# Empty TensorE instructions that move seven joined phases against lines of 256 instructions, and states' products first in four of them

## The chip, the cores and the metric

The kernel runs on one core of one Trainium2 chip. The metric is the device time of one execution in microseconds (us); lower is better. The core's engines run side by side, each through its own stream of instructions, and wait for each other by semaphores: TensorE (PE in the profile; its weight loads are PEld), VectorE (DVE), ScalarE (ACT), GpSimd (POOL) and SyncE (SP), which here starts nearly all DMAs. The median of three runs before the change is 552.23 us (550.72 to 553.09).

## What is computed

A linear-attention block, whose state decays step by step, is followed by a two-layer feed-forward block.

```python
# attention: r, k, v, w of (B=4, H=8, S=768, D=48), u of (H, D)
for t in range(S):
    cur = einsum('bhd,bhe->bhde', u[None] * kt, vt)
    y[:, :, t] = einsum('bhd,bhde->bhe', rt, state + cur)
    state = wt[:, :, :, None] * state + einsum('bhd,bhe->bhde', kt, vt)
x = y.transpose(0, 2, 1, 3).reshape(3072, 384)
# feed-forward: w_in of (384, 2048), w_out of (2048, 384)
h = x @ w_in
out = (h - tanh(h)) @ w_out
```

## The kernel before

**Blocks.** The 3,072 tokens are cut into eight blocks of 384 (`NB`): four sequences (`b`) of two halves (`q`). Loop `i` over the blocks runs the feed-forward part of block `i` and, between its steps, prepares the attention part of block `i + 1` (`later`). The attention of block 0 is done ahead, in `boot`.

**Feed-forward.** Inside a block, `f` runs over the 16 tiles of 128 hidden units. `first` (line 868) makes three matmuls, one for each 128 rows of `x`, into `hp`; its matmul is line 870. ACT copies `hp` to `h` (line 873), ACT and DVE make the activation `g` from it, and some tiles later the second layer consumes `g`. The second layer is done plainly in block 0 (`Second.add`, line 944, its matmul at line 947; in the last tiles of block 7 by `Second.added`, line 972) and by a scheme with fewer products in the others (`Fewer.product`, line 994), whose operands (`forms`, and sums of `g` tiles, line 917) DVE adds up. What is due is kept in the list `due`: the second layer of tile `f` is issued three tiles later in block 0, and from two tiles later on in the others.

**Attention.** A block is computed by chunks of 64 tokens (`L`). The products within a chunk form scores (line 493), which DVE copies under a mask to `A` (line 501) and to whose diagonal it copies another term (`diagonal_in`, line 396). The states at the chunks' starts come from products (line 574) that DVE adds and scales step by step (line 586). At tile 13 of blocks 0 and 1 and at tile 12 of blocks 2 to 6, `together` (line 731) joins both: `stretch` is called for `scores` and then for `from_state`, twice each, and makes up to 24 calls of a small matmul each time, all by line 756. In this text such a call of `together` is the joined phase of block `i`: it stands in the stream of block `i`, with the data of block `i + 1`. Where `later` is the first half of a sequence (`q` is 0, so `i` is 1, 3 or 5) the first chunk has no tokens ahead of it and the phase is shorter. ACT copies its results to `xT` and `late` (line 728), and small DMAs fill `xT` up.

Every matmul in float32 with line 870, 947, 994 or 756 stands in the profile as two matmuls and two weight loads. Thus three calls of line 870 make "x6".

**What sets the order.** PE, SP, DVE and ACT run in the order in which the program names their instructions; the order is written out by hand. In a tile `f` of a block, PE's order is: `first`, then phases of the attention part (line 493 or 574), then what is due of the second layer, then, in its tile, the joined phase. Where an instruction waits for more semaphores than it can hold, a separate semaphore instruction stands ahead of it in PE's stream. Behind the main part a branch leads, for inputs that don't keep to bounds checked on the way, to a general version of the whole computation (`general`), which also calls `first` and `Second.add`; with these inputs it isn't run.

Of the kernel before, what the change touches and what calls it, by code (L numbers as in the profile page):

```python
# [53 lines left out]
NB = 384  # L54
# [14 lines left out]
NF = FF // P  # L69
# [7 lines left out]
UNITS = [(0, 0), (0, 1)] + [u for j in range(NF // 2 - 2) for u in ((1, j), (0, j + 2))] + [(1, NF // 2 - 2),  # L77
                                                                                      (1, NF // 2 - 1)]
LATE = 3

# [43 lines left out]
def kernel(  # L126
# [12 lines left out]
    nc = tc.nc  # L139
# [76 lines left out]
    sums = const.tile([P, 16, P], F32, name="sums", tag="sums")  # L216

    def ring(t, at, n):
        return t[:, at + n % 4 * 3:at + n % 4 * 3 + 3].rearrange("p t c -> p (t c)")
# [3 lines left out]
    def g_at(q, x):  # L223
        if not isinstance(x, str):
# [9 lines left out]
    n_whole = blocks_n * NPAIR * NCH  # L234
    light = [n for n in range(blocks_n * NF) if NF - LATE <= n < blocks_n * NF - 2 and
             (n < NF or few[n // NF])]
# [76 lines left out]
    def begin_behind(ins, then):  # L313
        tc.add_manual_dep(then.ins, ins.ins.name, mybir.DependencyInfo(
            mybir.DependencyClass.Sync, mybir.DependencyReason.DATA))
# [3 lines left out]
    class Block:  # L319
# [411 lines left out]
        def together(self, ps):  # L731

            self.results(ps)
            yp, spread, St, ended = self.yp, isinstance(ps, Kept), states[self.q], {}

            def scores(p, c, h, par):
                toks = slice(64 * par, 64 * par + 64)
                return self.v[toks, c, p * D2 + h * D:p * D2 + (h + 1) * D], A[toks, h, p, c, :]

            def from_state(p, c, h, par):  # L740
                rows = slice(64 * h, 64 * h + D)
                return St[rows, p, 2 * c + par, 0:D], self.chunk("pre", p, 2 * c + par, spread)[rows]

            def stretch(of, cross):
                first = cross not in ended
                begun = set()
                for n in range(UP):
                    for c in range(NCP):
                        for h in range(2):
                            for x in range(2):  # L750
                                p, par = UP * n + x, x ^ cross
                                if of is from_state and not (self.q or c or par):
                                    continue
                                lhs, rhs = of(p, c, h, par)
                                e0, n0 = 64 * (h ^ x), (n * NCP + c) * L
                                done = nc.tensor.matmul(yp[x][e0:e0 + D, par, n0:n0 + L], lhsT=lhs, rhs=rhs,  # L756
                                                        start=first and (x, e0) not in begun, stop=True,
                                                        skip_group_check=True)
                                begun.add((x, e0))
                                if not first and len(begun) == 1:  # L760
                                    begin_behind(ended[cross], done)
                if first:
                    ended[cross] = nc.gpsimd.memset(ended_at, 0.0)
                    begin_behind(done, ended[cross])

            for of in (scores, from_state):
                for cross in range(2):
                    stretch(of, cross)
            self.result_out(ALL)
            self.fill_holes([nc.sync])  # L770
# [94 lines left out]
                self.update_any(ps, p0, self.tots[L])  # L865
            self.together(ps)

    def first(xT, f, hp):
        for kc in reversed(range(KC)):
            nc.tensor.matmul(hp, lhsT=w_in_sb[:, f, kc, :], rhs=xT[kc],  # L870
                             start=(kc == KC - 1), stop=(kc == 0))
        h = dense.tile([P, NB], F32, name="h", tag="h")
        return h, nc.scalar.activation(out=h, in_=hp, func=AF.Copy, scale=1.0 / UPSCALE)  # L873

    def product(out, in0, scalar, in1, op0):
        return lambda: nc.vector.scalar_tensor_tensor(out=out, in0=in0, scalar=scalar, in1=in1,  # L876
                                                      op0=op0, op1=ALU.mult)
# [42 lines left out]
    def any_h(h, g):  # L920
        s, qa = (dense.tile([P, NB], F32, name=name, tag=name) for name in ("s", "qa"))
        th, qb, big = (inp.tile([P, 2 * HALF], F32, name=name, tag=tag)[:, 0:NB]
                       for name, tag in (("th", "k"), ("qb", "r"), ("big", "w")))
        nc.scalar.activation(out=s, in_=h, func=AF.Square)
        nc.scalar.activation(out=qa, in_=s, func=AF.Square, bias=shift[:, 0:1])
        nc.scalar.activation(out=qb, in_=s, func=AF.Square, bias=shift[:, 1:2])
        nc.scalar.activation(out=th, in_=h, func=AF.Tanh)
        nc.scalar.activation(out=big, in_=s, func=AF.Relu, bias=shift[:, 2:3])
        nc.vector.tensor_tensor(out=th, in0=h, in1=th, op=ALU.subtract)
        product(h, h, SERIES, s, ALU.mult)()  # L930
        product(h, qa, QUAD[0][1], h, ALU.add)()
        product(g, qb, QUAD[1][1], h, ALU.add)()
        nc.vector.copy_predicated(out=g, mask=big.bitcast(I32), data=th)
        return g

    def places(at, n):
        return sums[:, at:at + n].rearrange("p n c -> p (n c)")

    class Second:
# [1 line left out]
        def __init__(self, row0, acc, first=0):  # L941
            self.row0, self.acc, self.first = row0, acc, first

        def add(self, f, g):
            for j in range(NB // P):
                acc = self.acc[j][:, 0:DM]
                nc.tensor.matmul(acc, lhsT=g[:, j * P:(j + 1) * P], rhs=w_out_sb[:, f, :],  # L947
                                 start=(f == self.first), stop=(f == NF - 1))
                if f == NF - 1:
                    rows = slice(self.row0 + j * P, self.row0 + j * P + P)  # L950
                    if rows.stop == N:
                        for at, engine in ((slice(0, DM // 2), nc.scalar), (slice(DM // 2, DM), nc.vector)):
                            o = places(12, 3)[:, at]
                            if engine is nc.scalar:
                                nc.scalar.activation(out=o, in_=acc[:, at], func=AF.Copy, scale=1.0 / UPSCALE)
                            else:
                                nc.vector.tensor_single_scalar(o, acc[:, at], 1.0 / UPSCALE, op=ALU.mult)
                            queue = nc.scalar if engine is nc.scalar else nc.sync
                            queue.dma_start(out=out[rows, at], in_=o)
                        continue  # L960
                    o = dense.tile([P, DM], F32, name="o", tag="o", bufs=2) if j < 2 else places(12, 3)
                    nc.scalar.activation(out=o, in_=acc, func=AF.Copy, scale=1.0 / UPSCALE)  # L962
                    nc.sync.dma_start(out=out[rows, :], in_=o)
# [245 lines left out]
    xT = blocks[0].begin()  # L1209
# [32 lines left out]
    for i, blk in enumerate(blocks):  # L1242
        here = xT
        later = blocks[i + 1] if i + 1 < len(blocks) else None
        after = blocks[i + 2] if i + 2 < len(blocks) else None
        if later:
            xT = later.begin()
# [3 lines left out]
        second = Second(row0, acc, few[i]) if few[i] < NF else None  # L1251
        for f in range(NF):
# [2 lines left out]
                op()  # L1255
            spare_a, spare_b = (t[:, 0] for t in ps_a.both)
            to = [acc[0], acc[1], hp, spare_a, spare_b, spare_a][now] if now < 6 else hp
            h, made = first(here, f, to[:, 0:NB])
            if not i:
                made_up = converting(pieces, (PIECES[f] if f < len(PIECES) else 1) - 1)  # L1260
                for op in ahead_of_h:
# [2 lines left out]
            g, ahead_of_h, square, later_ops = slight(h, now, i, f)  # L1264
            some = ({4: (0, 2), 6: (2, 4), 8: (4, 6), 9: (6, 8), 14: (8, len(SUMS))} if later else
                    {4: (0, 4), 6: (4, 8), 8: (8, len(SUMS))}).get(f) if summed else None
            spare = summed[0].sum(*some) if some else []
# [76 lines left out]
            for name in loads.get(f, ()):  # L1344
                of, ins = (after if name in ("w", "k", "r") else later), None
# [34 lines left out]
    with tc.If(anew > 0, label="anew"):  # L1380
        with tc.manual_schedule(engines={PE, SP, DVE, ACT}), ExitStack() as again_pools:
            ps_d = again_pools.enter_context(tc.tile_pool(name="ps_e", bufs=1, space=PSUM))
            ps_a = again_pools.enter_context(tc.tile_pool(name="ps_b", bufs=2, space=PSUM))
            acc = [ps_d.tile([P, BANK], F32, name=f"acc{j}", tag=f"acc{j}") for j in range(NB // P)]
            hp = ps_d.tile([P, NB], F32, name="hp", tag="hp")
            draw((1, 2, 4, 8), slice(128, 288))
            for st in states:
                nc.vector.memset(st[:, :, :, D:], 0.0)
            for blk in [Block(b, q) for b in range(B) for q in range(NQ)]:
                blk.general(ps_a)  # L1390
                second = Second(blk.b * S + blk.q * NB, acc)
                for f in range(NF):
                    second.add(f, any_h(first(blk.xT, f, hp)[0], ring(sums, 0, f)))


# [52 lines left out]
```

## Time and profile before

| | |
|---|---|
| median of 3 runs | 552.23 us (550.72 to 553.09) |
| profiled execution | 552.88 us; span 551.1 us |
| PE busy | 536.8 us (97%), 5,682 matmuls |
| PEld busy | 404.7 us (73%) |
| DVE busy | 459.3 us (83%) |
| ACT busy | 403.6 us (73%) |
| granted TensorE clock | 0.995 mean |
| DMA | 56.29 MB, mean 102 GB/s |

The span runs from the first to the last instruction of the profiled execution, whose time lies a little above the median of the three runs. A row of a group or timeline names line, engine, operation and tile (out<-in), and in brackets or behind a bar the idle time ahead with what ended it. "issue" there means that the engine waited for nothing that the profile shows. The rows by stage give, for each engine, busy microseconds and the count of instructions, then the granted clock, the DMA engines' busy share and GB/s. "PEldq" marks instructions that PE's sequencer runs itself.

### The profile page before, as it was taken

The page shows a single profiled execution, that of the slowest core. Times are in us where ns is not written, and L with a number is a line of the kernel's source. Part 1 is how long each engine was busy: PE and PEld are TensorE (multiplying, and loading weights), DVE is VectorE, ACT ScalarE, POOL GpSimd, SP SyncE. Part 2 cuts the span into 40 slices and gives each one's busy share as a digit, 9 for nine tenths or more (in the row PEclk, how much of TensorE's full clock was granted, in tenths as well). Part 3 has the DMA queues.
Part 4 walks back from the last instruction along what each step waited for, and adds up shares of the span by engine and source line. Part 5 has one row for each costly group of instructions (what it writes and reads, how often), then busy time and mean ns, then how long its engine had stood idle before and what let it go on. Part 6 is the DMA issues. An engine that isn't in the chain of part 4 may idle for free.

```text
span 551.1 us, 14091 instructions
## 1 busy us (share of the span) xinstructions
PE 536.8 (97%) x5682; PEld 404.7 (73%) x5682; DVE 459.3 (83%) x943; ACT 403.6 (73%) x814; POOL 6.5 (1%) x47
## 2 busy tenths in 40 slices
PE   8999989999999999999999999999999999999996
PEld 5756655677777787878777787777877777787874
DVE  7899997899979989799897889879787897557563
ACT  5899975897568886688666887588855986666561
POOL 1100000000000000000000000000000000000000
PEclk9999998999999999999999999999999999999999
DMA  7798632252302532144112532126222320200101
GB/s 273 256 398 320 216 116 70 86 129 75 118 11 87 113 113 92 57 122 138 61 55 50 139 117 66 50 87 160 66 86 63 82 63 2 56 0 1 45 1 46
DMA packets 53045, 56.29 MB, mean 102 GB/s; under 512 B 21488, under 2 KB 50928, under 8 KB 52976
## 3 DMA queue, kind: packets, MB, share of 16 engines
q1 hardware_dynamic: 52592, 55.18, 32.8%
q8 instruction: 45, 0.74, 0.6%
q14 instruction: 24, 0.20, 0.1%
q10 hardware_dynamic: 288, 0.10, 0.1%
q0 software_dynamic: 96, 0.07, 0.1%
HBM read 44.73 MB, written 4.72 MB: 90 GB/s over the span
## 4 chain that ended last, share of the span: by engine, by line
PE 92%; DVE 4%; issue 2%; DMA 1%; SPq 0%; DVEq 0%
PE hp L870 43%; PE acc L994 26%; PE att L994 6%; PE acc L947 5%; PE att L756 4%; PE att L493 2%; PE acc L972 2%; PE att L574 2%; PE att L870 1%; DMA r<-in_rT 1%; PE acc L870 1%; DVE scores L501 1%; DVE first_states L630 0%; DVE pre L416 0%; DVE w_sb L267 0%
## 5 line engine op out<-in xcount | busy, mean ns | idle before, releaser
L870 PE MATMUL hp<-xT,w_sb 128*128 128x384 f32 x738 | 260.1, 489 | 0.0
L870 PEld LDWEIGHTS hp<-xT,w_sb 128*128 128x128 f32 x738 | 132.1, 191 | 69.4 <-issue 0.3
L994 PE MATMUL acc<-forms,g 128*128 128x128 f32 x954 | 133.2, 276 | 0.0
L873 ACT ACTIVATE h<-hp 128x384 f32<-128x384 f32 x123 | 60.2, 489 | 98.8 <-PE hp L870 98.3
L994 PEld LDWEIGHTS acc<-forms,g 128*128 128x128 f32 x954 | 122.0, 192 | 10.3
L876 DVE SCALAR_TENSOR_TENSOR h<-h,s 128x384 f32<-128x384 f32 x128 | 70.6, 551 | 60.4 <-ACT s L891 60.4
L917 DVE TENSOR_TENSOR g<-g 128x256 f32<-128x256 f32 x265 | 103.1, 418 | 7.4 <-PE acc L994 6.5
L892 ACT ACTIVATE qa<-s,shift 128x384 f32<-128x384 f32 x113 | 69.5, 615 | 3.7
L894 ACT ACTIVATE junk<-s,shift 128x384 bf16<-128x384 f32 x113 | 67.7, 599 | 0.0
L876 DVE SCALAR_TENSOR_TENSOR g<-qa,h 128x384 f32<-128x384 f32 x112 | 61.5, 550 | 1.6 <-ACT qa L902 0.2
L891 ACT ACTIVATE s<-h 128x384 f32<-128x384 f32 x113 | 59.1, 523 | 3.6
L994 PEld LDWEIGHTS acc<-w_sb,g 128*128 128x128 f32 x318 | 46.8, 191 | 9.7 <-ACT sums L962 0.3
L994 PE MATMUL acc<-w_sb,g 128*128 128x128 f32 x318 | 53.0, 276 | 0.0
L994 PE MATMUL att<-w_sb,g 128*128 128x128 f32 x212 | 35.5, 275 | 0.0
L994 PEld LDWEIGHTS att<-w_sb,g 128*128 128x128 f32 x212 | 31.1, 192 | 5.3
L947 PE MATMUL acc<-w_sb,sums 128*128 128x384 f32 x96 | 34.6, 498 | 0.2 <-DVE sums L876 0.2
L1029 DVE TENSOR_TENSOR sums<-sums 128x256 f32<-128x256 f32 x84 | 32.7, 405 | 1.7 <-ACT sums L1006 1.4
L263 ACT ACTIVATE up<-raw 128x768 f16<-128x768 f32 (+1 forms) x32 | 32.9, 1061 | 0.0
L947 PEld LDWEIGHTS acc<-w_sb,sums 128*128 128x128 f32 x96 | 18.6, 196 | 13.5 <-DVE sums L876 1.1
L416 DVE TENSOR_TENSOR_SCAN pre<-w,start 128x780 f32<-128x780 f32 x14 | 24.9, 1782 | 0.8
L428 DVE TENSOR_TENSOR_SCAN post<-w,seed 128x780 f32<-128x780 f32 x14 | 24.8, 1775 | 0.0
L894 ACT ACTIVATION_READ_ACCUMULATOR junk<-s,shift 128x1 f32 x113 | 21.1, 187 | 0.0
(118 smaller groups left out, 530.1 us busy)
## 6 DMA issues: line engine op xcount, KB each, us to landing
raw<-in_weights SPq DMA_DIRECT2D x16, 768.0 KB, 6.3
w<-in_wT SPq DMA_DIRECT2D x7, 780.0 KB, 4.5
k<-in_kT SPq DMA_DIRECT2D x7, 768.0 KB, 4.7
r<-in_rT SPq DMA_DIRECT2D x7, 768.0 KB, 4.5
v_sb<-in_v SPq DMA_DIRECT2D x8, 576.0 KB, 4.0
k<-in_tokens SPq DMA_DIRECT2D x7, 576.0 KB, 3.9
r<-in_tokens SPq DMA_DIRECT2D x7, 576.0 KB, 4.7
out_y<-sums SPq DMA_DIRECT2D x18, 128.0 KB, 1.8
```

The lines of the kernel that those rows point to most:

```text
L263: return lambda: nc.scalar.activation(out=to, in_=of, func=AF.Copy, scale=scale, bias=bias)
L416: return nc.vector.tensor_tensor_scan(out=self.tile("pre")[:, cols], data0=self.tile("w")[:, cols], data1=start[:, 0:n * NCH * LP], initia ...
L870: nc.tensor.matmul(hp, lhsT=w_in_sb[:, f, kc, :], rhs=xT[kc], start=(kc == KC - 1), stop=(kc == 0))
L873: return h, nc.scalar.activation(out=h, in_=hp, func=AF.Copy, scale=1.0 / UPSCALE)
L876: return lambda: nc.vector.scalar_tensor_tensor(out=out, in0=in0, scalar=scalar, in1=in1, op0=op0, op1=ALU.mult)
L891: nc.scalar.activation(out=s, in_=h, func=AF.Square)
L892: nc.scalar.activation(out=qa, in_=s, func=AF.Square, bias=shift[:, 4:5])
L894: nc.scalar.activation(out=junk[:, 0:NB], in_=s, func=AF.Relu, bias=shift[:, 5:6], accum_out=excess[:, at:at + 1])
L917: return lambda: nc.vector.tensor_tensor(out=G[:, to:to + 2], in0=two(G, g_at(q, a0), g_at(q, a1)), in1=two(G, g_at(q, b0), g_at(q, b1)), ...
L947: nc.tensor.matmul(acc, lhsT=g[:, j * P:(j + 1) * P], rhs=w_out_sb[:, f, :], start=(f == self.first), stop=(f == NF - 1))
L994: nc.tensor.matmul(to, lhsT=G[:, g_at(q, a), :], rhs=rhs, start=start, stop=stop, skip_group_check=True)
L1029: ops.append(lambda op=op, at=at: nc.vector.tensor_tensor(out=at[0], in0=at[1], in1=at[2], op=OPS[op]))
```

## The change

Three things are edited. A table `SPACED` gives, for each block, how many empty instructions (`nc.tensor.nop`) `first` issues behind each of its three matmuls: one number for the tiles up to 13 (blocks 0 and 1) or 12 (the others), one for the tiles behind. `Second.add` issues one behind each of its matmuls in block 0 for tiles 0 to 10. The two calls in the general version ask for none. In `together`, `from_state` goes ahead of `scores` where `self.q` is 1, that is in blocks 0, 2, 4 and 6; elsewhere the order stays.

```diff
+SPACED = (3, 0), (0, 3), (3, 2), (2, 3), (3, 2), (2, 3), (3, 0), (0, 0)
...
-            for of in (scores, from_state):
+            for of in (from_state, scores) if self.q else (scores, from_state):
                 for cross in range(2):
                     stretch(of, cross)
...
-    def first(xT, f, hp):
+    def first(xT, f, hp, apart=0):
         for kc in reversed(range(KC)):
             nc.tensor.matmul(hp, lhsT=w_in_sb[:, f, kc, :], rhs=xT[kc],
                              start=(kc == KC - 1), stop=(kc == 0))
+            for _ in range(apart):
+                nc.tensor.nop(nofuse=True, hint="apart")
...
-        def add(self, f, g):
+        def add(self, f, g, spare=True):
             for j in range(NB // P):
                 acc = self.acc[j][:, 0:DM]
                 nc.tensor.matmul(acc, lhsT=g[:, j * P:(j + 1) * P], rhs=w_out_sb[:, f, :],
                                  start=(f == self.first), stop=(f == NF - 1))
+                if self.row0 == 0 and f < NF - 5 and spare:
+                    nc.tensor.nop(nofuse=True, hint="apart")
...
-            h, made = first(here, f, to[:, 0:NB])
+            h, made = first(here, f, to[:, 0:NB], SPACED[i][f > 12 + (i < 2)])
...
-                    second.add(f, any_h(first(blk.xT, f, hp)[0], ring(sums, 0, f)))
+                    second.add(f, any_h(first(blk.xT, f, hp)[0], ring(sums, 0, f)), False)
```

## The prediction

> **What bounds the kernel now.** I read the page first, for the chain of work that ended last; then the list of what TensorE (PE) waited for.
>
> ```profile
> PE 92%; DVE 4%; issue 2%; DMA 1%; SPq 0%; DVEq 0%
> ```
>
> ```profile
> PE att L756 <- issue: 4.8, 4, 1.7
> ...
> PE att L756 <- DVE scores L396: 1.4, 1, 1.4
> ```
>
> PE is the bound nearly everywhere, so time taken from it reaches the end. Behind the start-up its waits are almost all in one place: line 756, the joined phases, of which there are seven, one in each of blocks 0 to 6. Four of them hold a wait for "issue", time in which nothing that the profile shows was missing; one holds a wait for VectorE (DVE). The timeline of PE has the places (start, length, count; the idle time ahead in brackets), first in block 0, then the rows that end the other three waits.
>
> ```profile
> 75.19 2.20 PE L947 MATMUL acc<-w_sb,sums 128*128 128x384 f32 x6 [0.19 <-DVE sums L876]
> 78.82 1.56 PE L756 MATMUL att<-scores,v_sb 64*48 64x64 f32 x96 [1.43 <-DVE scores L396]
> 80.20 1.41 PE L756 MATMUL att<-pre,states 48*48 48x64 f32 x85
> 83.26 0.42 PE L756 MATMUL att<-pre,states 48*48 48x64 f32 x11 [1.66 <-issue]
> ...
> 150.26 0.59 PE L756 MATMUL att<-pre,states 48*48 48x64 f32 x23 [1.08 <-issue]
> ...
> 276.03 0.42 PE L756 MATMUL att<-pre,states 48*48 48x64 f32 x10 [0.71 <-issue]
> ...
> 405.43 0.44 PE L756 MATMUL att<-pre,states 48*48 48x64 f32 x15 [1.35 <-issue]
> ```
>
> All four fall near the end of a phase, with 11, 23, 10 and 15 matmuls to go. Is the distance between them regular in instructions? The view of busy time by stage counts matmuls (PE) and weight loads (PEld) from one such end to the next, and the view of a line lists the separate semaphore instructions, here between the second and the third (x6, x2, x2) and between the first and the second (x3, x2).
>
> ```profile
> 83.26:150.26 67.00, 65.93 (x638) 47.31 (x637) 60.74 (x121) 50.49 (x107) 0.58 (x5) 0.97 0.35 98
> 150.26:276.03 125.77, 125.06 (x1403) 98.51 (x1403) 111.10 (x228) 94.67 (x199) 0.64 (x8) 1.00 0.31 87
> 276.03:405.43 129.40, 128.05 (x1403) 100.71 (x1403) 111.47 (x232) 95.95 (x202) 0.64 (x8) 1.00 0.32 89
> ```
>
> ```profile
> L870 PEldq EVENT_SEMAPHORE  x6: 51/51/198, 154.2 to 220.9; - x6
> ...
> L994 PEldq EVENT_SEMAPHORE  x2: 51/51/51, 169.7 to 233.5; - x2
> ...
> L574 PEldq EVENT_SEMAPHORE  x2: 51/51/51, 199.5 to 263.4; - x2
> ...
> L870 PEldq EVENT_SEMAPHORE  x3: 51/51/51, 87.4 to 92.1; - x3
> ...
> L994 PEldq EVENT_SEMAPHORE  x2: 51/51/51, 103.6 to 103.7; - x2
> ```
>
> 1,403 + 1,403 + 10 = 2,816 = 11 x 256, twice; and 638 + 637 + 5 is 1,280 = 5 x 256. No larger number divides both. So each wait ends exactly where a new line of 256 instructions begins. The view of DMA from 401 to 408 us shows that line arriving (40 slices of 0.175 us).
>
> ```profile
> GB/s 369 211 114 0 0 0 0 0 94 0 0 0 0 0 0 0 0 0 0 0 0 0 0 0 0 0 0 0 0 0 0 94 0 0 0 0 0 0 0 0
> ...
> q8 instruction: 2, 0.03, 2.3%
> ```
>
> Two instruction packets: one at about 402.5, 2.9 us ahead of the resumption at 405.43; the next at about 406.5, 1.1 us behind it. Entering a line thus seems to ask for the following one, which is usable about 4 us later. Ordinary lines last far longer. A joined phase does not:
>
> ```profile
> 146.74:150.78 4.04, 2.96 (x177) 2.74 (x176) 3.94 (x9) 1.06 (x3) 0.18 (x2) 1.00 0.02 6
> 208.64:211.47 2.83, 2.83 (x194) 2.75 (x193) 2.83 (x6) 1.06 (x3) 0.18 (x2) 1.00 0.06 15
> 272.60:276.38 3.78, 3.07 (x177) 2.84 (x176) 3.78 (x8) 1.06 (x3) 0.18 (x2) 1.00 0.02 5
> 337.51:340.34 2.83, 2.83 (x193) 2.75 (x193) 2.83 (x6) 1.06 (x3) 0.18 (x2) 1.00 0.03 9
> 401.47:405.80 4.33, 2.98 (x177) 2.75 (x177) 4.33 (x10) 1.07 (x3) 0.18 (x2) 1.00 0.02 4
> 466.93:469.76 2.83, 2.83 (x194) 2.75 (x193) 2.21 (x6) 1.06 (x3) 0.18 (x2) 1.00 0.03 6
> ```
>
> A clean phase issues 192 pairs, 384 instructions, in 2.83 us: 7.4 ns each, so a line wholly inside it is eaten in 1.9 us. Phases 1, 3 and 5 have 176 pairs, 352 instructions (the first 64 tokens of a sequence have none ahead of them). From the matmuls left, the boundary stalls at instruction 384 - 22 = 362 of phase 0, and 306, 332 and 322 of phases 1, 3 and 5; the line before begins 256 earlier, at 106, 50, 76 and 66: inside. For the clean phases the same count runs from the last boundary to the phase:
>
> ```profile
> 150.26:208.50 58.24, 58.23 (x517) 45.55 (x517) 51.88 (x107) 45.49 (x96) 0.14 (x2) 1.00 0.32 88
> 276.03:337.36 61.33, 61.33 (x522) 47.85 (x522) 51.81 (x109) 46.76 (x99) 0.14 (x2) 1.00 0.35 94
> 405.43:466.78 61.35, 61.35 (x527) 47.88 (x527) 50.77 (x109) 44.68 (x95) 0.00 (x0) 1.00 0.21 55
> ```
>
> With five waits each (one block, half of the ten above), 1,039, 1,049 and 1,059 instructions, that is 15, 25 and 35 over a multiple of 256: the line began that far ahead of the phase, the next lies 241, 231 and 221 inside, and one more, 256 on, does not fit. No line is wholly inside, and there is no wait. Fifteen slow instructions ahead are enough.
>
> **The empty instructions: where they put the phases.** Each takes one place in PE's stream and no array. Counted from the diff, ahead of phase 0 come 14 first-layer tiles x 3 matmuls x 3 = 126 and 11 second-layer tiles x 3 = 33: 159. Tiles 14 and 15 of block 1 add 18, each of blocks 2, 4 and 6 adds 13 x 9 = 117 ahead of its phase, blocks 3 and 5 add 78, and the tails add 18, 27, 18, 27. Ahead of phases 0 to 6 that makes 159, 159, 294, 390, 534, 630 and 774. The first boundary inside (106, 50, 241, 76, 231, 66, 221) moves forward by as much, modulo 256: to 203, 147, 203, 198, 209, 204 and 215. Every line that holds the start of a phase then begins 41 to 109 instructions ahead of it, and the second boundary, 256 on, lies beyond 384 everywhere. So all four waits should go, and the three clean phases stay clean with more room than before.
>
> **What that is worth.** Phases 1, 3 and 5 should take 2.83 x 352/384 = 2.59 us, and take 4.04, 3.78 and 4.33: 1.45 + 1.19 + 1.74 = 4.4 us. Behind phase 0 the clock falls as well; the chain in order of time has the first-layer matmuls behind phase 0, and behind clean phase 2:
>
> ```profile
> 83.69 3.04 PE hp L870 x6
> 86.73 2.72 PE acc L947 x6
> 89.45 1.94 PE hp L870 x6
> ...
> 211.54 2.13 PE hp L870 x6
> ```
>
> Phase 0 lasts from 78.82 to 83.69, 4.87 instead of 2.83: 2.0 us. Then 3.04 - 2.13 plus 2.72 - 1.94 is 1.7 us, which goes if PE no longer stands still there. The Trainium skill, TensorE: Matmul & The Clock Gate, "What's actually happening", says that the gate judges PE in free-running windows of 3.4 us; by that rule the dip need not come in every execution, and the sum for one without it would be 1.7 us less. The trace has this one dip in mid-kernel and none behind the three shorter waits.
>
> **The price of the empty instructions.** 774 of them, on PE's sequencer. The trace of before has none; nearest are the semaphore instructions above, 51 ns each. Upper bound: all in the path, 774 x 0.051 = 39.5 us. Lower bound: nothing, and not below, since they do no work. I take nothing: three stand among the first-layer matmuls at the head of every block, and PE's count of waits shows no gap at line 870. The cover is the matmuls: a call of line 870 holds PE 1.94/3 = 0.65 us and three empty instructions hold the sequencer 0.15. Without that cover (an empty queue) they would cost their full 51 ns.
>
> **The swap.** In blocks 0, 2, 4 and 6 the states' products go ahead of the scores'. In block 0 PE stands 1.43 us for the scores, while the states are long there: the first row below has their last start, 61.8; the second is the last of block 2, the third the scores' in block 0.
>
> ```profile
> L586 DVE TENSOR_TENSOR states<-states,whole x6: 348/358/360, 57.7 to 61.8; 128x192 f32<-128x192 f32 x6
> ...
> 206.12 0.36 DVE L586 TENSOR_TENSOR states<-states,whole 128x192 f32<-128x192 f32 x1
> ...
> 76.86 1.91 DVE L396 COPY_PREDICATED scores<-mask_all,diagonal 128x768 f32<-128x768 uint8 x2
> ```
>
> PE is free at 75.19 + 2.20 = 77.39; the states' half lasts 2.83/2 = 1.4 us, to 78.8; the scores are ready at 76.86 + 1.91 = 78.77. So 1.4 us go. In block 2 the states are done at 206.48, 2.2 us ahead of the phase at 208.64: no new wait, and if there were one, it would hold ACT's copy of the results and the next first-layer matmuls behind it. No DMA is issued elsewhere; those behind the phase come earlier with it.
>
> **Sum.** 4.4 + 2.0 + 1.7 + 1.4 = 9.5 us. The profiled execution took 552.88 (its span 551.1 and 1.8 around it): 543.4. The median shown is 0.65 lower and would give 542.7. Of what is earlier, DVE is late next: between 84 and 112 us it waits 5.2 us, all on ACT, and phase 0 with its dip and its wait brings PE forward by 5.1.
>
> ```profile
> DVE h L876 <- ACT s L891: 5.2, 6, 1.6
> ```
>
> So its reserve there is spent almost whole, and I allow 0.5 us for it: **543.2**.
>
> **Rivals.** (1) DVE becomes the bound in blocks 0 and 1: PE waits in second-layer matmuls for g. For: the reserve above is as large as the gain. Against: g is consumed two or three tiles, some 8 us, behind its making. If half of the 5.1 is lost: 546. (2) The waits are no fetches, or the empty instructions do not take places as counted: then only the swap's 1.4 us is left, perhaps with the dip: 552.2 - 1.4 = 550.8, or 549.1. Against it stand the counts above. The Trainium skill, Runtime: NRT & Kernel Launch, "Instruction fetch mechanics", tells of blocks of 256 instructions, as counted here, and says that their fetch is hidden because issue is slower; by that rule this rival holds. The trace disagrees where the issue runs at 7.4 ns. (3) Slower: an empty instruction is no free passenger, PE's queue runs dry behind it, each time. It decides from 9.5/774 = 12 ns each on; at the full 51 ns the time is 552.2 - 9.5 + 39.5 = 582. Against: the semaphore instructions at line 870 leave no gap. For: there are never more than three of those close together, and here come nine in a tile. (4) The line-up is right in the count but a phase slips by a constant: 41 instructions of room where it is least (phase 6), so one or two waits could return, near 1.5 us each with the phase's loss: 545 to 546.
>
> **How the numbers follow.** Forecast 543.2: 0.72, its own range 541.2 (lowest run 550.7 less 9.5) to 544.9 (if the dip's 1.7 stays). Rival 1: 0.10. Rival 4: 0.05. Rival 2: 0.06. Rival 3: 0.07. The range, 541 to 547.5, holds the forecast, rivals 1 and 4; the cases left out are 0.13. A measurement of this kernel can tell about 0.5%, 2.8 us, from no change: faster than 549.4 are the forecast, rivals 1 and 4 and a little of rival 2, 0.88; same, the rest of rival 2, 0.05; slower 0.07.
>
> **What would show it.** Right: no wait for issue at line 756; phases of 2.83 and 2.59 us; the states' row ahead of the scores' in block 0 and no wait for line 396; a clock of 1.00 from 77 to 90 us; line 870 at 1.94 us a tile with its empty instructions; a span near 541.7. Wrong: a gap at line 870, or its rows of six matmuls above 2.10 us away from the phases (rival 3), issue waits at other places of the phases (rivals 2 and 4), waits of lines 947 and 994 for DVE around 85 to 115 us (rival 1). A time above 549.4 overturns the forecast.

## The result, and the profile after

| | before | after |
|---|---|---|
| median, runs of one chip | 551.70 us (550.72 to 553.09, 4 runs) | 544.70 us (544.35 to 545.07, 4 runs) |
| ratio | | 0.9877 [0.9856, 0.9898] |
| profiled execution | 552.88 us | 545.07 us; span 543.3 us |
| PE busy | 536.8 us (97%) | 534.1 us (98%) |
| DVE busy | 459.3 us (83%) | 459.0 us (84%) |
| granted TensorE clock | 0.995 | 1.000 |

The kernel became 7.0 us faster by the medians and 7.8 us by the two profiled executions; 9.0 were forecast. Lines have moved: the joined phases' matmul is now line 757, the first layer's 871, block 0's second layer 950, `diagonal_in` 397.

The first fence is the whole list of what PE waited for in the kernel after (engine, tile, line, what it waited for: us in total, times, longest).

```profile
PE att L312 <- POOL ident masks.py:199: 2.1, 1, 2.1
PE att L494 <- ACT k L454: 0.8, 1, 0.8
PE hp L871 <- ACT h L876: 0.4, 1, 0.4
PE att L679 <- PEq L717: 0.3, 1, 0.3
PE att L697 <- DVE states L632: 0.2, 1, 0.2
```

Neither the four waits for issue nor the wait for the scores is left, and no second-layer line waits for DVE. The view of busy time by stage has the seven joined phases (from:to, length, then busy us and instructions of PE, PEld, DVE, ACT and POOL, the clock, the share of the DMA engines, GB/s):

```profile
78.24:81.35 3.11, 3.04 (x193) 2.85 (x192) 3.11 (x5) 1.61 (x4) 0.18 (x2) 1.00 0.73 225
142.78:145.54 2.76, 2.76 (x177) 2.68 (x177) 2.69 (x6) 1.06 (x3) 0.18 (x2) 1.00 0.04 9
203.39:206.22 2.83, 2.83 (x193) 2.76 (x192) 2.83 (x6) 1.06 (x3) 0.18 (x2) 1.00 0.02 8
267.36:270.12 2.76, 2.76 (x177) 2.69 (x176) 2.76 (x5) 1.06 (x3) 0.18 (x2) 1.00 0.03 7
331.25:334.09 2.84, 2.84 (x194) 2.76 (x193) 2.84 (x6) 1.06 (x3) 0.18 (x2) 1.00 0.04 10
395.22:397.99 2.77, 2.77 (x178) 2.69 (x177) 2.77 (x5) 1.06 (x3) 0.18 (x2) 1.00 0.03 8
459.11:461.94 2.83, 2.83 (x193) 2.76 (x192) 2.22 (x6) 1.06 (x3) 0.18 (x2) 1.00 0.02 6
```

Phases 1, 3 and 5 fell from 4.04, 3.78 and 4.33 us to 2.76 and 2.77; 2, 4 and 6 are what they were. The chain of work that ended last, in order of time, shows phase 0 and the tiles behind it:

```profile
78.31 1.49 PE att L757 x96
79.80 0.07 issue
79.86 1.56 PE att L757 x96
81.42 2.13 PE hp L871 x6
83.56 1.94 PE acc L950 x6
85.49 1.94 PE hp L871 x6
```

The first layer behind the phase starts at 81.42 instead of 83.69, and its next tile at 85.49 instead of 89.45: the six matmuls take 2.13 and 1.94 us, so the clock no longer falls here. The empty instructions stand in the views of lines 874 (`first`) and 953 (`Second.add`): count, then shortest, median and longest in ns.

```profile
L874 PEldq NOP  x741: 13/13/13, 23.3 to 455.9; - x186
...
L953 PEldq NOP  x33: 13/13/13, 30.1 to 76.3; - x33
```

741 + 33 = 774, the number counted from the diff. Each record lasts 13 ns, but the starts of successive ones lie mostly 71 ns apart.

**Where the time came from.** Each row is the change of one distance between PE's rows, from the last first-layer tile ahead of the phase (for the dip: the tile just behind it) to the next tile behind, in us against the profiled execution of before. The kernel after was profiled three times; the other two stand in the experiments.

```
                              after  after_again  after_third
phase 0 with its wait         -3.26     -3.15        -3.17
fall of the clock behind it   -1.69     -1.69        -1.69
phase 1                       -1.29     -1.28        -1.29
phase 3                       -1.02     -1.02        -1.02
phase 5                       -1.56     -1.57        -1.56
sum                           -8.82     -8.71        -8.73
```

In the first of them 1.0 us of the 8.8 was lost again ahead of phase 0. The timeline of ACT and then that of PE show where: a copy of weights waits for its load, `h` of tile 7 comes late behind it, and the first layer waits.

```profile
36.59 0.92 ACT L264 ACTIVATE w_sb<-raw 128x768 f32<-128x768 f32 x1 [0.85 <-DMA raw<-in_weights]
```

```profile
47.33 2.20 PE L871 MATMUL hp<-xT,w_sb 128*128 128x384 f32 x6 [0.38 <-ACT h L876]
```

8.8 - 1.0 = 7.8, the difference of the two profiled executions.

### The profile page after: what moved, and what is told of

It is laid out like the page before. It is cut to its first block, busy times and chain, and to the rows that moved or that the text cites. A ratio compares the mean times of both kernels' runs of the same rounds, so it can differ in the third digit from the quotient of the medians.

```text
span 543.3 us, 14866 instructions
## 1 busy us (share of the span) xinstructions
PE 534.1 (98%) x5682; PEld 403.3 (74%) x5682; DVE 459.0 (84%) x943; ACT 403.7 (74%) x814; POOL 6.5 (1%) x47
## 4 chain that ended last, share of the span: by engine, by line
PE 88%; DVE 6%; ACT 2%; issue 2%; DMA 1%; SPq 0%; DVEq 0%
PE hp L871 41%; PE acc L999 27%; PE att L999 7%; PE att L757 4%; PE acc L950 3%; PE acc L977 2%; PE att L494 2%; PE att L575 1%; PE att L871 1%; ACT up L264 1%; DMA r<-in_rT 1%; DVE w_sb L268 1%; PE acc L871 1%; DVE scores L502 1%; DVE states L587 1%
```

## The experiments

Two theories stood against each other at first. By the first, PE stands still when a line of 256 instructions lies wholly inside a joined phase, since the phase eats it before the next has come; the empty instructions move the lines. By the second, the gain comes from the swap, and the waits are something else. Medians are given beside those of the kernel before on the same chip.

**The swap alone** (the kernel before with this edit):

```diff
-            for of in (scores, from_state):
+            for of in (from_state, scores) if self.q else (scores, from_state):
```

> The kernel before with the swap alone, no empty instructions. Theory (the waits for issue are lines of 256 instructions that lie wholly inside a joined phase): they stay where they were in the stream, with 22, 46, 20 and 30 instructions to go in phases 0, 1, 3 and 5; only the 1.4 us wait for the scores goes: 1.4 us less than before, or 3.1 less if the clock's dip behind phase 0 needs both halts. Rival (the waits come from the order of the two products): the waits for issue go or change place, 5 us or more less.

Measured: 553.76 us (10 runs) beside 552.23 (13 runs), ratio 1.0016 [0.9994, 1.0037]: no gain, where the theory had 1.4 us less. The timeline of PE has phase 0:

```profile
80.64 1.56 PE L756 MATMUL att<-pre,states 48*48 48x64 f32 x96
82.26 1.45 PE L756 MATMUL att<-scores,v_sb 64*48 64x64 f32 x85
86.13 0.42 PE L756 MATMUL att<-scores,v_sb 64*48 64x64 f32 x11 [2.43 <-issue]
```

The states go first and the wait for the scores is gone, but the issue wait, again with 11 to go, grew from 1.66 to 2.43 us. The matmuls behind the wait are now the other operands': it belongs to the place in the stream, not to the data. Phases 1, 3 and 5, which the swap doesn't touch, kept their waits (1.41, 1.02 and 1.12 us). Why the one in phase 0 grew is taken up in the experiment with the loads.

**The empty instructions alone** (the kernel after with the swap undone):

```diff
-            for of in (from_state, scores) if self.q else (scores, from_state):
+            for of in (scores, from_state):
```

> The changed kernel with the order of the products undone, empty instructions kept. Theory: no wait for issue in any joined phase, phases 1 and 3 and 5 at 2.76 us; the wait of 1.4 us for the scores in block 0 stays; no dip of the clock, since one halt of 1.4 us is shorter than the waits of phases 1 and 5 that had none behind them: 1.0 to 1.4 us more than the changed kernel. Rival (order): the waits come back, 4 us or more above the changed kernel.

Measured: 546.10 us (4 runs) beside 552.23, ratio 0.9882 [0.9847, 0.9917]. The timeline of PE in phase 0:

```profile
78.85 1.56 PE L757 MATMUL att<-scores,v_sb 64*48 64x64 f32 x96 [1.43 <-DVE scores L397]
```

This is the only wait left at line 757. Empty instructions carry nearly all of the gain; with the swap on top, phase 0 gains 3.15 to 3.26 us instead of the 1.88 of this profile. The 1.0 to 1.4 us more than after that the theory gave can't be told from the ratios (0.9882 and 0.9877). The clock did not fall behind the 1.43 us wait, as expected, but the reason given for that doesn't hold: the waits of phases 1 and 5 in the kernel before, 1.08 and 1.35 us, were not longer.

**Nearly as many empty instructions in other places** (before, with 673 of them):

```diff
+PADS = 20, 0, 161, 91, 155, 91, 155, 0
+def pads(i, f, kc):
+    at, n = f * 3 + kc, 36
+    return PADS[i] * (at + 1) // n - PADS[i] * at // n if at < n else 0
...
-    def first(xT, f, hp):
+    def first(xT, f, hp, i=None):
...
+            for _ in range(0 if i is None else pads(i, f, KC - 1 - kc)):
+                nc.tensor.nop(nofuse=True, hint="apart")
...
-            h, made = first(here, f, to[:, 0:NB])
+            h, made = first(here, f, to[:, 0:NB], i)
```

They are spread over the first 36 calls of line 870 of a block so that every joined phase, the three clean ones too, holds a whole line.

> The kernel before with other numbers of empty instructions (20 in block 0, 161 in block 2, 91 in 3, 155 in 4, 91 in 5, 155 in 6), so that in all seven joined phases one line lies wholly inside. Theory: seven waits for issue, each ending at the boundary counted: instruction 343 of phase 0, 286 of phase 1, 316 of the others, so with about 20, 33, 34, 18, 34, 18, 34 matmul pairs to go. Phases 2, 4 and 6, clean before, take 3.8 to 4.4 us instead of 2.83: 3 to 5 us above the kernel before. Rival (empty instructions help wherever they stand, as a pause or by making room): waits go or shrink, time at or below the kernel before.

Measured: 556.59 us in one run, beside 552.23. The timeline of PE (the matmul's line is 762 here):

```profile
83.78 0.54 PE L762 MATMUL att<-pre,states 48*48 48x64 f32 x21 [1.87 <-issue]
...
147.06 1.82 PE L762 MATMUL att<-pre,states 48*48 48x64 f32 x80
...
210.13 0.76 PE L762 MATMUL att<-pre,states 48*48 48x64 f32 x34 [1.01 <-issue]
...
275.33 0.53 PE L762 MATMUL att<-pre,states 48*48 48x64 f32 x18 [0.87 <-issue]
...
340.43 0.76 PE L762 MATMUL att<-pre,states 48*48 48x64 f32 x34 [1.05 <-issue]
...
405.64 0.53 PE L762 MATMUL att<-pre,states 48*48 48x64 f32 x18 [0.88 <-issue]
...
471.02 0.76 PE L762 MATMUL att<-pre,states 48*48 48x64 f32 x34 [1.34 <-issue]
```

Phases 2, 4 and 6, clean before, now wait, with the 34 matmuls to go that the count gives; 0, 3 and 5 wait with 20 (a record more here), 18 and 18 to go. In phase 1 no wait is listed, but the row of its states is 1.82 us long, where 1.45 is undisturbed. The timeline of the weight loads (PEld) has the wait inside it, with the 33 to go that were forecast:

```profile
148.12 0.62 PEld L762 LDWEIGHTS att<-pre,states 48*48 48x48 f32 x33 [0.29 <-issue]
```

So all seven waits stand where the count put them; why this one is so much shorter isn't shown. An empty instruction neither removes nor makes a wait; where it puts the line does both.

**The price of empty instructions** (the kernel after, with more in block 7, which has no joined phase):

```diff
-            h, made = first(here, f, to[:, 0:NB], SPACED[i][f > 12 + (i < 2)])
+            h, made = first(here, f, to[:, 0:NB], SPACED[i][f > 12 + (i < 2)] if i < 7 else 6 if f < 5 else 24 if f < 10 else 0)
```

> The changed kernel with more empty instructions in block 7, behind all joined phases: 6 behind each first-layer matmul in tiles 0 to 4, 24 in tiles 5 to 9. In the trace of the changed kernel they follow each other on PE's sequencer every 0.071 us. Theory (they cost the sequencer's time, hidden while it is shorter than the matmuls): 18 x 0.071 = 1.3 us in a tile of 3.27 us, so tiles 0 to 4 don't change; 72 x 0.071 = 5.1 us, so tiles 5 to 9 take 5.1 us or a little more instead of 3.27, 7 to 10 us in all less what the queue holds. Rival (free however many): no change anywhere. Rival (each one stops the array): tiles 0 to 4 longer by 0.9 us or more each.

Measured: 557.91 us in one run, 12.8 above the profiled execution of after; some of it is a fall of the clock at 517 us, behind the waits that this edit makes. The timeline of PE has two tiles with six behind each matmul, then calls with 24:

```profile
483.71 2.10 PE L871 MATMUL hp<-xT,w_sb 128*128 128x384 f32 x6
...
486.98 2.10 PE L871 MATMUL hp<-xT,w_sb 128*128 128x384 f32 x6
...
490.26 0.81 PE L871 MATMUL hp<-xT,w_sb 128*128 128x384 f32 x2
491.52 0.88 PE L871 MATMUL hp<-xT,w_sb 128*128 128x384 f32 x2 [0.45 <-issue]
493.29 0.88 PE L871 MATMUL hp<-xT,w_sb 128*128 128x384 f32 x2 [0.89 <-issue]
```

With six, the tiles start 3.27 us apart and their matmuls stay at 2.10 us: 18 a tile cost nothing. With 24, calls start 1.77 us apart, 74 ns for each, near the 71 ns of the records. Tiles 5 to 8 take 5.4 to 6.2 us, a little more than the 5.1 counted, and the whole loss is above the 7 to 10 us expected, even without the fall of the clock (about 1.7). So an empty instruction takes 0.07 us of the sequencer, and the matmul ahead of it covers it: 6 x 0.07 = 0.42 us fit under a call's 0.65, 24 don't. The change has at most three.

**After again, the empty instructions again, and the early ones moved** (on one chip). The first two are the kernels above once more; the first also asks whether the 1.0 us lost in block 0 is the price of its 159 empty instructions. The third moves the start-up, too, against the lines: it shifts the stream ahead of all tiles, in the attention of block 0, by 63 more of the 16 x 16 matmuls that `boot` issues there already (`spare`) and four fewer of the longer ones behind them (`ahead`), and leaves one empty instruction behind each first-layer matmul and none in `Second.add`.

```diff
-SPACED = (3, 0), (0, 3), (3, 2), (2, 3), (3, 2), (2, 3), (3, 0), (0, 0)
+SPACED = (1, 0), (0, 3), (3, 2), (2, 3), (3, 2), (2, 3), (3, 0), (0, 0)
...
-                if self.row0 == 0 and f < NF - 5 and spare:
-                    nc.tensor.nop(nofuse=True, hint="apart")
...
-        own = blk.own(ps, h1, spare=94, ahead=5, late=6)
+        own = blk.own(ps, h1, spare=157, ahead=1, late=6)
```

> The changed kernel once more, beside its version with the products' order undone (the run below). Theory (the waits saved are the joined phases' alone; the 1.0 us that its first profile lost in tiles 6 to 8 of block 0 was a late DMA of weights): 544.5 to 545, and in its profile tiles 0 to 13 of block 0 start within 0.4 us of the kernel before. Rival (empty instructions in block 0 cost 1 us): the same loss in the same tiles.

> The changed kernel with the order of the products undone, again. Theory (with the lines out of the way, the swap is worth the wait for the scores): 1.1 to 1.4 us above the run beside it. Rival (the swap is worth nothing with or without empty instructions): within 0.4 us.

> The changed kernel with the start-up moved against the lines as well: 63 more filler matmuls of 16 columns and 4 fewer wide ones ahead of the first scores, so 118 instructions more there, and for it one empty instruction behind each first-layer matmul of block 0 instead of three and none behind the second layer; the joined phases keep their places within 2. The shortest line of the start-up then lasts about 3.5 us instead of 2.9. Theory: no wait for issue at line 494, joined phases as in the changed kernel, and the time 0 to 0.5 us below it, as the start-up stalls in some executions alone. Rival (the clock needs the wide fillers): the start-up at half clock, 1 us or more above.

Measured, beside 551.70 (11 runs): 545.37 us for after (6 runs), 0.9876 [0.9852, 0.9901]; 545.81 without the swap (6 runs), 0.9880 [0.9856, 0.9903]; 546.11 with the early ones moved (6 runs), 0.9885 [0.9861, 0.9909]. In the second profile of after, block 0 lost nothing at tiles 6 to 8, with the same 159 empty instructions: the loss in the first was a load that came late, not their price. Its tile 0 started at 24.05 us, though, against 23.50 in the first and 23.42 before, and tiles 1 to 13 some 0.8 us later than before, where at most 0.4 was expected. So the start-up moves an execution by 0.6 us here, and a late load by 0.9 in the first. That also hides the swap: in phase 0 it gains 1.1 us between this pair of profiles (-3.15 against -2.07), but 0.4 by these medians, between the theory's 1.1 to 1.4 and the rival's nothing. Moving the early ones was a miss: 0.7 us above after, where 0 to 0.5 below was expected. The list of PE's waits shows what it did:

```profile
PE att L494 <- issue: 0.5, 1, 0.5
...
PE att L697 <- issue: 0.3, 1, 0.3
```

It gave the start-up issue waits of its own, and tile 0 started at 24.89.

**The swap with other loads.** In the swap alone, the view of DMA from 82 to 85 us (40 slices of 0.075 us) shows the engines full up to 83.7; the view of 83.6 to 83.8 has the instruction packet.

```profile
DMA  8789999999999999999999931100000000000000
```

```profile
q8 instruction: 1, 0.02, 30.6%
```

The line that holds PE up was asked for from instruction 106 of the phase on, at 80.64 + 106 x 0.0074 = 81.4 us: its packet came 2.3 us later, behind a load of `k` of 768 KB. In the kernel before, the line was asked for at 78.82 + 0.78 = 79.6 us, and the view of 79 to 84 us (slices of 0.125 us) has its packet at 80.8, just as a load ends:

```profile
DMA  9999999999974250000000000000000000000000
```

If the load makes the wait longer, another order of the loads should shorten it:

```diff
-            loads.update({2: "next r", 11: "w", 13: "k", 14: "r"})
+            loads.update({2: "next r", 11: "w", 14: "k", 15: "r"})
```

> The swap alone, as in swap_only, with block 0's loads of k and r issued one tile later, behind the joined phase instead of into it. Theory (the line fetched in phase 0 queued behind the 768 KB of k, so the swap's gain was given back): the wait for issue in phase 0, still with 11 pairs to go, is 0.7 to 1.4 us instead of 2.43, and the phase lasts 3.9 to 4.4 us instead of 5.85. Rival (the load has nothing to do with it; the fetch takes what it takes from the phase's start): 2 us or more, phase above 5.2 us.

Measured: 550.83 us in one run, beside 551.70. The timeline of PE in phase 0, and the view of DMA from 80 to 84 us (slices of 0.1 us):

```profile
79.05 1.56 PE L756 MATMUL att<-pre,states 48*48 48x64 f32 x96
80.68 1.45 PE L756 MATMUL att<-scores,v_sb 64*48 64x64 f32 x85
83.21 0.42 PE L756 MATMUL att<-scores,v_sb 64*48 64x64 f32 x11 [1.08 <-issue]
```

```profile
DMA  0000060000000000000000000000000000000000
```

The engines are idle but for the instruction packet at 80.5, 0.7 us after the line was asked for (79.05 + 0.78 = 79.8), and the wait fell from 2.43 to 1.08 us, at the same instruction. The phase, 4.51 us, was a little above the 3.9 to 4.4 expected. So this is where the swap's gain went in the profile of the swap alone: PE no longer waited for the scores, but the packet stood behind the load, and the wait for the line took back part of it. Measured as in the table above, phase 0 gains 0.43 us with the swap alone and 1.75 with the loads moved as well, though the line still lies inside; with them moved, the clock doesn't fall behind the phase either. The swap alone's 3.2 us above the profiled execution of before are its start-up, which the swap doesn't edit: an issue wait of 1.5 us at line 493, a clock of 0.50 behind it, and tile 1 starting 3.3 us later. Whether its other nine runs had that too isn't shown.

**Another way: the joined phase in two halves.** Instead of moving the lines, this version (with the swap, without empty instructions) issues the second half one tile later, so that no stretch is long enough for a whole line.

```diff
...
-            for of in (scores, from_state):
-                for cross in range(2):
+            for n, of in enumerate((from_state, scores) if self.q else (scores, from_state)):
+                for cross in range(2) if part in (None, n) else ():
                     stretch(of, cross)
-            self.result_out(ALL)
-            self.fill_holes([nc.sync])
+            if part != 0:
+                self.result_out(ALL)
+                self.fill_holes([nc.sync])
...
-            if later and "results" in phases.get(f, ()):
-                later.together(ps_a)
+            for part in range(2):
+                if later and "results" in phases.get(f - part, ()):
+                    later.together(ps_a, part)
```

> No empty instructions and no attention to where the lines fall: the swap, and each joined phase cut into its two halves, the second half and the results' copies one tile later, behind that tile's matmuls of both layers. Theory (a wait needs 256 instructions issued faster than a line arrives): a half has 192 instructions at most and some 3.3 us of large matmuls behind it, so no wait for issue at the joined phases and no wait for the scores; each second half costs the 0.1 to 0.2 us of one more change of tile shape, as the matmuls behind a phase show (2.13 us instead of 1.94): 1.0 to 1.5 us above the changed kernel, 5 us or more below the one before. Rival (the waits belong to these matmuls, however they are placed): waits for issue in the second halves, time at 550 or above.

> The changed kernel once more, on the chip of the run beside it: 544.5 to 545.5, without a wait for issue at the joined phases.

Measured on one chip: 550.32 us for the halves (10 runs), ratio 0.9957 [0.9926, 0.9988]; 544.58 for after (4 runs), 0.9869 [0.9824, 0.9914]; before 552.20 (13 runs). The halves' list of PE's waits:

```profile
PE hp L873 <- DMA xT<-late: 2.1, 5, 0.6
...
PE att L493 <- issue: 1.3, 1, 1.3
```

The joined phases hold no wait for issue, as the theory has it. But the time is 5.7 us above after, where 1.0 to 1.5 was expected. The results leave a tile later, and the small DMAs that fill `xT` end too late for the first tiles of blocks 1 and 2; by PE's rows some 3.5 us more than in the first profile of after go there. Phases 1 to 6 take 0.2 to 0.3 us more each (0.1 to 0.2 was expected), and the start-up 1 us more, with an issue wait of its own and a clock of 0.50 behind it. No version that was tried beats the changed kernel.

## Why the prediction was right, and where its sizes were off

**The waits.** That they are the ends of fetches of 256-instruction lines was right, and so was the line-up: PE's instructions, counted in the trace of after from the same start as before, put the first boundary inside phases 0 to 6 at 204, 146, 202, 197, 208, 203 and 214, where 203, 147, 203, 198, 209, 204 and 215 were forecast. One reading was loose: a line is not usable "about 4 us" after it is asked for. From the instruction that asks for it to the end of the wait it is 3.7, 3.2, 2.9 and 3.5 us in the four waits of before. The sum doesn't use it. Rivals 2 and 4 fall with the line-up; the Trainium skill's rule that fetch is hidden (Runtime: NRT & Kernel Launch, "Instruction fetch mechanics") doesn't hold where the issue runs at 7.4 ns and PE waits up to 2.43 us.

**Phases 1, 3 and 5** were mis-sized: 4.4 us forecast, 1.29 + 1.02 + 1.56 = 3.9 measured. The step that failed is "2.83 x 352/384 = 2.59". Phases with 176 pairs take 2.76, so their time isn't in proportion to the pairs; 3 x 0.17 = 0.5 us. The scores' half takes 1.38 us there as in a clean long phase, but so do the 80 pairs of the states' half, where 96 take 1.45. Why these are slower isn't shown.

**Phase 0 and the swap**: 2.0 + 1.4 = 3.4 forecast, 3.2 measured. The timelines of DVE and PE in the kernel after show what is missing:

```profile
77.78 1.94 DVE L397 COPY_PREDICATED scores<-mask_all,diagonal 128x768 f32<-128x768 uint8 x2
```

```profile
78.24 1.56 PE L757 MATMUL att<-pre,states 48*48 48x64 f32 x96
79.86 1.56 PE L757 MATMUL att<-scores,v_sb 64*48 64x64 f32 x96
```

The scores are ready at 77.78 + 1.94 = 79.72, and the second half starts 1.62 us behind the first instead of 1.38: 0.24 us still go to them, and the phase takes 3.11 us instead of 2.83. The experiments add what the prediction didn't see: what the swap is worth hangs on the wait for the line behind it. By itself it brought 0.43 us in phase 0 and nothing by the medians; with the lines moved 1.1 to 1.4 in phase 0, and with the loads moved instead, the phase gained 1.75, 0.58 of it the shorter wait for the line (1.08 against 1.66).

**The fall of the clock**: 1.7 forecast, 1.69 between these two traces. But it was counted whole against the median. Of the 11 executions of before in one batch, six had a mean clock of 1.000, with times of 551.16 to 552.42 (median 551.4), and five one of 0.991 to 0.998, 551.44 to 554.75. An execution of before without the fall, about 551.4, less 8.8 - 1.7 = 7.1 is 544.3, and the kernel after took 544.58 to 545.37. That the 551.4 ran without the fall is read from their clock; none of them has a trace.

**The empty instructions** at nothing: right. Six behind one matmul are as free as three, and rival 3's condition, an empty queue, was met only with 24.

**DVE**: rival 1's premise was right, its end wrong. DVE's wait for ACT in this stretch (now 80 to 108 us) fell from 5.2 us to

```profile
DVE h L879 <- ACT s L894: 0.6, 1, 0.6
```

and yet no second-layer matmul waited for it. The allowance of 0.5 us was not needed there. The start-up and a late load took more than that, and the prediction foresaw neither; that the allowance brought the forecast nearer to the time is luck.

In short: the sum of 9.5 was 8.8; 0.5 of the difference is the short phases and 0.2 phase 0. The rest of the distance to the medians is the clock's fall, which before doesn't have every time, and the way to phase 0, on which the three profiles of after lost 0.7 to 1.0 us against before.

## What to carry to other kernels

Where many small matmuls follow one another at 7.4 ns an instruction, count the instructions from one unexplained wait to the next: if the distances share a large factor, the wait is the stream itself, and a few empty instructions behind long matmuls, at 0.07 us each and free while shorter than the matmul, move it to where it costs nothing. Check that move by its opposite, with about as many empty instructions that put the lines wrong. And a swap that removes one wait is worth only the distance to the next limit behind it, here a fetch that stood behind a bulk load.

## What the runs showed of the hardware

- A fetch of instructions comes later behind bulk loads. With a load of 768 KB under way the packet came 2.3 us after the line was asked for and PE waited 2.43 us; with one near its end 1.2 and 1.66 us; with the DMA engines idle 0.7 and 1.08 us.
- Which wait makes the clock fall isn't told by its length. With the lines put wrong, the view by stage has the time behind phase 0 (waits of 1.44 and 1.87 us in it) and that behind phase 6 (one wait of 1.34 us):

```profile
83.78:90.00 6.22, 6.22 (x39) 3.89 (x39) 5.92 (x11) 3.85 (x9) 0.00 (x0) 1.00 0.11 26
471.90:475.40 3.50, 3.50 (x6) 1.79 (x6) 0.00 (x0) 1.54 (x4) 0.00 (x0) 0.51 0.11 26
```

  The clock stayed at 1.00 behind the longer waits and fell to 0.51 behind the single short one. That agrees with the free-running windows of the Trainium skill (TensorE: Matmul & The Clock Gate, "What's actually happening"), by which the place of a wait in its window counts. Each fall in these traces between the start-up and the last tiles lasts 3.4 us, and the one in the start-up of the swap alone 6.8.
- The start-up has issue waits of its own in some executions: 0.2 us in one profile of after and none in the other two, 0.5 and 0.3 with the early ones moved, 1.5 in the swap alone, 0.7 with its loads moved and 1.3 in the halves. In the last three the clock fell to 0.50 there, first in the swap alone and then with its loads moved:

```profile
21.85:28.68 6.83, 6.59 (x99) 5.02 (x97) 4.43 (x10) 3.26 (x5) 0.13 (x2) 0.50 0.98 357
23.05:26.46 3.41, 3.33 (x51) 2.52 (x52) 1.85 (x5) 2.19 (x4) 0.00 (x0) 0.50 0.95 332
```

  Why these three have it isn't shown.
